# Hedgehog attention into a spectral mode mix: 19 groups of the mix attached to listed iterations of the attention in place of 22 to consecutive ones

## The chip, the cores and the metric

The kernel runs on 1 core of one Trainium2 chip. The metric is the device time of one execution in microseconds (us). Engines: PE is TensorE (matmul; PEld its weight loads), DVE is VectorE, ACT is ScalarE, POOL is GpSimd, SP is SyncE; transfers are issued by SP and POOL and carried by 16 DMA engines. Each engine works through its own queue in order.

## What is computed

Two stages, the second on the result of the first. Shapes: 8 batches, 8 heads, 576 positions, head size 64, model size 512, 64 modes.

```python
def phi(x):                                   # attention with a feature map
    proj = np.einsum('bhsd,df->bhsf', x, w_phi)
    proj = proj - np.max(np.abs(proj), axis=-1, keepdims=True)
    return np.concatenate([np.exp(proj), np.exp(-proj)], axis=-1)
q_p, k_p = (phi(q), phi(k))
kv  = np.einsum('bhsf,bhsd->bhfd', k_p, v)
z   = np.sum(k_p, axis=2)
num = np.einsum('bhsf,bhfd->bhsd', q_p, kv)
den = np.einsum('bhsf,bhf->bhs', q_p, z)[..., None] + 1e-06
x   = num / den                               # heads side by side: 8 x 576 x 512

X = np.fft.rfft(x, axis=1)                    # the spectral mode mix
Xr, Xi = (np.real(X[:, :n_modes]), np.imag(X[:, :n_modes]))
Yr = np.einsum('bmd,mde->bme', Xr, w_r) - np.einsum('bmd,mde->bme', Xi, w_i)
Yi = np.einsum('bmd,mde->bme', Xr, w_i) + np.einsum('bmd,mde->bme', Xi, w_r)
Y[:, :n_modes] = Yr + 1j * Yi
y = np.fft.irfft(Y, n=S, axis=1)
u = x + y
out = u + np.maximum(u @ w_ch, 0.0)
```

`w_r` and `w_i` are 64 matrices of 512 x 512 each, float32: 134 MB to be read, out of the 163.6 MB that the kernel reads in all.

## The kernel before

**Attention.** One loop (L555) over n = 0 to 33. Step n begins the n-th of 32 units `S` (two heads of one batch, or one head of two batches for the first 8), goes on with unit n - 1 (`prev`) and ends unit n - 2 (`old`), all in an order written out by hand. For the present unit: features on PE (`feat_tok`, `feat_q`, `rem_mm`), their maxima on DVE (`absmax`, `mkq`), exponentials on ACT (`exps`, `ekq`), v scaled on POOL (`vscale`, tile `vaug`). For `prev`: `kv_mm`, `num_mm` on PE, the division on DVE (`numer`), which writes x in bfloat16 into `xs_all`. For `old`: `x_mm`, the forward transform on PE, which ACT copies into one of two tiles, `XT0` or `XT1` (L369). In steps 28 to 33 a first part of x W (`flip_early`, `times_w_early`) is added for 6 of the 40 blocks of x.

**Which unit fills which tile.** Units 0 to 3 fill `XT1`, 4 to 7 `XT0`, 8 to 15 (g = 1) `XT1`, 16 to 23 (g = 2) `XT0`, 24 to 31 (g = 3) `XT1`; unit n is written in step n + 2.

**Mode mix.** 32 groups (L108). Groups 0 to 7 take 16 modes of 64 input rows each; groups 8 to 31 take 8 modes `gi` of 128 input rows, g = 1, 2, 3. `weights(k)` (L156) issues a group's `wr` and `wi` from POOL, read as float32 and written as bfloat16 (two transfers of 1 MB written, or four of 0.5 MB for groups 0 to 7), into one of `NW = 3` buffers. `mode_mm(k)` (L390) multiplies (16 or 32 matmuls of 512 columns, `wr` first), `mode_sum(k)` (L424) adds the result to `Yacc` on DVE, or, for g = 3, writes the sum `yst`. `after` (L111) is the last unit that a group's tile needs.

In the loop, a step that has a group does `mode_mm` at its end; the next step does `mode_sum` near its start and then issues the weights of the group three further on:

```python
            while k_in < min(k_out + NW, 2 if n < 3 else 32):   # L585
                weights(k_in)
                k_in += 1
```

On POOL these issues stand behind `load_qk` (q and k of two units, in odd steps 5 to 25) and in front of `vscale` of the step; `wr` waits until PE has read the old `wr` of that buffer, `wi` likewise. `wchb` (`w_ch`) is loaded by POOL in step 16; v (`vn`) by SP two steps ahead.

**Which step has which group** (L622): group k goes to the first step that is free from `after[k] + 2` on, while k < 22. That is groups 0 to 7 in steps 5 to 12, 8 to 15 in 17 to 24, 16 to 21 in 25 to 30.

**After the attention** (L785) a loop over the groups left, k = 22 to 31. For each: the issue of weights three further on, `mode_mm`, `mode_sum`; for g = 3 a `times_w`, four transposes of `yst` (`ptY`, copied to `sY`), and with every odd `gi` `by_batch` (`psZY`, whose copies to `zy` by ACT and DVE are done in the pieces that follow, L717). Then `pieces(plan[k])`: each piece is a `flip_x` (transposes of a pair of blocks of x, `pt`, copied by DVE to `sT`) and a `times_w` (8 matmuls, `psW`, copied by ACT to `xw`), 17 pairs in all. Then up to two `reordered` (L685: `psX` on PE, copied back to `xs_all` by ACT), for k <= 24 and for even k, 11 in all; a block is reordered only after it was flipped. For k = 30 one `times_w` more closes the list; for k = 31 `add_xw` (`psB`) goes ahead of `mode_mm`.

**The end** (L841): 20 units of output: matmuls that add x W, Y W and the inverse transform in PSUM, ReLU on ACT (L762), sum on DVE (L776), in part POOL (L780), and the stores.

Of the kernel before, what the change touches and what calls it, by code (L numbers as in the profile page):

```python
# [26 lines left out]
def kernel(  # L27
# [63 lines left out]
    def qk_pair(pool, i):  # L91
        return [pool.tile([128, 2, 10, D_], BF16, name=f"{nm}2_{i}") for nm in "qk"]
# [18 lines left out]
    after = [3] * 4 + [7] * 4 + [15] * 8 + [23] * 8 + [31] * 8  # L111
    W = {}

    def load(st, which="qkv"):
        for nm, src, bufs in (("q", q, 2), ("k", k, 2), ("v", v, 4)):
            if nm not in which or (nm != "v" and st["n"] >= 2):
                continue
            pool = pa_in if nm == "v" else pa_first
            t = pool.tile([128, 9, D_], F32, name=f"{nm}n", tag=f"{nm}n", bufs=bufs)
            if "bs" in st:  # L120
                for x in range(2):
                    nc.sync.dma_start(  # L122
                        t[64 * x:64 * x + 64],
                        src[st["bs"][x], st["h"]].rearrange("(p j) d -> p j d", j=9))
            else:
                b, g = st["b"], st["g"]
                nc.sync.dma_start(
                    t, src[b, 2 * g:2 * g + 2].rearrange("h (p j) d -> (h p) j d", j=9))
            st[nm] = t


    def load_qk(m):
        st = S[2 * m]
        for nm, src, t in zip("qk", (q, k), qk2s[m % 3]):
            if "bs" in st:
                for x in range(2):
                    b = st["bs"][x]
                    nc.gpsimd.dma_start(
                        t[64 * x:64 * x + 64, :, 0:9, :],
                        src[b:b + 3:2, st["h"]].rearrange("u (p j) d -> p u j d", j=9))  # L140
            else:
                b, g = st["b"], st["g"]
                nc.gpsimd.dma_start(
                    t[:, :, 0:9, :],
                    src[b:b + 2, 2 * g:2 * g + 2].rearrange("u h (p j) d -> (h p) u j d", j=9))
            for x in range(2):
                S[2 * m + x][nm + "b"] = t[:, x]

    def casts(st, eng, which="qk"):
        n = st["n"]  # L150
        for nm, t in zip("qk", qk2s[0]):
            if nm in which:
                st[nm + "b"] = t[:, n % 2]
                eng.tensor_copy(t[:, n % 2, 0:9, :], st[nm])
# [39 lines left out]
    def feat_tok(st, nm, tag):  # L194
        ps = psum.tile([128, 2, 4, 128], F32, name=f"ps{nm}", tag=tag, bufs=1)
        for c in range(4):
            for jj in range(2):
                r = slice(64 * jj, 64 * jj + 64)
                nc.tensor.matmul(ps[:, jj, c, :], lhsT=st[nm + "T"][r, c, :], rhs=w2[r, :],  # L199
                                 start=True, stop=True)  # L200
        st["ps" + nm] = ps
# [248 lines left out]
    def zeros(i):  # L450
        for z in (0, 32, 64):
            nc.vector.memset(XTs[i][:, z:z + 16, :], 0.0)
# [71 lines left out]

    psY = None
    k_in = k_out = 0
    K_IN_ATTN = 22
    pa_last_cm = None
    with tc.manual_schedule():
        load(S[0], "qk")  # L530
        setup()
        load(S[0], "v")
        load(S[1])
        zeros(1)
        casts(S[0], nc.vector)
        casts(S[1], nc.gpsimd, "q")
        load_qk(1)
        for t in AAs:
            nc.gpsimd.memset(t[:, 0, :, 1152:1216], 1.0)
        for t in e2s:  # L540
            nc.gpsimd.memset(t[64:128, :, NCH - 1:NCH], 1.0)
        casts(S[1], nc.gpsimd, "k")

        pa_first_cm.__exit__(None, None, None)
        pa_last_cm = tc.tile_pool(name="pa_last", bufs=1)
        pa_last = pa_last_cm.__enter__()
        qk2s[2] = qk_pair(pa_last, 2)
        for t in qk2s[2]:
            nc.gpsimd.memset(t[:, :, 9, :], 0.0)
        load_qk(2)  # L550
        weights(0)
        k_in = 1
        transp(S[0], "q")
        transp(S[0], "k")
        for n in range(N + 2):  # L555
            cur = S[n] if n < N else None
            prev = S[n - 1] if 0 <= n - 1 < N else None
            old = S[n - 2] if 0 <= n - 2 < N else None
            nxt = S[n + 1] if n + 1 < N else None
            if n + 2 < N:  # L560
                load(S[n + 2])
            if cur:
                feat_tok(cur, "k", "pB")
                feat_q(cur)
            if psY is not None:
                mode_sum(k_out, psY)
                psY = None
                k_out += 1
            if cur:
                rem_mm(cur)  # L570
                absmax(cur, "k")
                absmax(cur, "rem")
                exps(cur, "q")
            if nxt:
                transp(nxt, "q")
            if prev:
                kv_mm(prev)
                kv_cp(prev)
            if cur:
                ekq(cur, "k")  # L580
            if n < 4:
                vscale(cur)
            if n % 2 == 1 and 5 <= n < N - 5:
                load_qk((n + 5) // 2)
# [3 lines that stand above are left out]
            if n in (1, 3):  # L588
                load_qk((n + 5) // 2)
            if n == 16:  # L590
                nc.gpsimd.dma_start(wchb, moe_w_ch.rearrange("(dc p) e -> p dc e", p=128))
            if cur and n >= 4:
                vscale(cur)
            if nxt:
                transp(nxt, "k")
            if cur:
                exps(cur, "k")
                exps(cur, "rem")
            if prev:
                num_mm(prev, 1)  # L600
                numer(prev, 0)
                num_mm(prev, 0)
                numer(prev, 1)
                numer(prev, 2)
            if old:
                x_mm(old)
            e = n - (N + 2 - N_EARLY)
            if e >= 0:
                sTe = flip_early(e)
            if cur:  # L610
                feat_tok(cur, "q", "pA")
                absmax(cur, "q")
                ekq(cur, "q")
            if n == 0:
                forward_matrix()
            if n == 2:
                zeros(0)
            if 10 <= n < 10 + NCH:
                inverse_matrix(n - 10)
            if e >= 0:  # L620
                times_w_early(e, sTe)
            if k_out < K_IN_ATTN and n >= after[k_out] + 2:  # L622
                psY = mode_mm(k_out)
    if psY is not None:
        mode_sum(k_out, psY)
# [157 lines left out]
    u0 = dict(bc=((0, 0), (0, 1)), half=False, late=False, tags=("T2", "T3"))  # L783

    with tc.manual_schedule():  # L785
        plan = {22: 3, 23: 3, 24: 2, 25: 2, 26: 2, 27: 1, 28: 2, 29: 1, 30: 1, 31: 0}
        while k_out < 32:
            k = k_out
            gi = groups[k][1]
            while k_in < min(k_out + NW, 32):  # L790
                weights(k_in)
                k_in += 1
            if k == 31:
                add_xw(u0)
            yst = mode_sum(k, mode_mm(k, "T3"), pb)
            k_out += 1
            if yst is not None:
                if ahead:
                    times_w()
                if gi % 2 == 0:  # L800
                    sY = pb.tile([128, 4, 2, 128], BF16, name="sY", tag="sY")
                for a, b, tag in ((0, 4, "T3"),) if k < 31 else ((0, 2, "T0"), (2, 4, "T1")):
                    pt = psum.tile([128, b - a, 128], BF16, name="ptY", tag=tag)
                    for dc in range(a, b):
                        nc.tensor.transpose(pt[:, dc - a, :], yst[dc], ident_b)
                    nc.vector.tensor_copy(sY[:, a:b, gi % 2, :], pt)
                if k == 31:
                    add_x(u0)
                if gi % 2 == 1:
                    by_batch(sY, gi // 2)  # L810
            pieces(plan[k])
            if k <= 24 or k % 2 == 0:
                assert not copies
                for tag in ("T0", "T1"):
                    if reorder:
                        reordered(tag)
            if k == 30:
                times_w()
        assert not todo and not ahead and not reorder and not copies
# [67 lines left out]
```

## Time and profile before

| what | value | where from |
|---|---|---|
| time, median of 3 runs | 456.05 us (455.77 to 456.72) | runs |
| span of the profiled execution | 456.7 us | page |
| busy: PE, DVE, ACT, POOL | 66%, 64%, 57%, 44% | page, part 1 |
| POOL's DMA queue: bytes written | 76.75 MB | page, part 3 |
| read from HBM, written to it | 163.64 MB, 9.44 MB | page |
| step 5, 10, 11, 21, 31 begin (`psT`) | 53.7, 94.0, 114.6, 196.2, 312.9 us | trace |
| groups 8, 21, 22, 30, 31 begin on PE | 170.7, 310.4, 331.1, 402.8, 415.6 us | trace |
| `wi` of groups 19, 22, 30, 31 lands | 291.2, 322.2, 404.6, 414.4 us | trace |
| waits of PE for `wi` at L416 | 29.6 us, 12 times | waits |
| waits of PE for `wr` at L416 | 8.7 us, 3 times | waits |
| from the end of group 31 (416.7 us) to the end | 40.0 us | trace |

How to read it: every time is counted from the first instruction of the profiled execution. A share of busy time is an average over stages; the steps, groups and landings in the lower rows place the stages. A transfer "lands" when its semaphore says so. The granted clock of PE is 1.00 at full speed.

### The profile page before, as it was taken

Reading aid. Unit: us, or ns where it says so; the run is one execution under the profiler, and the core shown is the slowest. Engines: PE = TensorE matmul, PEld = TensorE weight load, DVE = VectorE, ACT = ScalarE, POOL = GpSimd, SP = SyncE. Lnnn points to the kernel's source line nnn. Section 1 sums busy time; section 2 is a strip of 40 time slices with the busy share of each in tenths; the row PEclk is TensorE's granted clock in tenths of the full one; section 3 lists DMA queues with packets and bytes.
Section 4 is the critical chain, followed back from the end, with each engine's and each line's share of the span. In section 5 each row is a group of like instructions: output and inputs, shape, how many; then the busy total and the mean of one; then the engine's idle time right before and its main releaser. Section 6 shows DMA issues by size and latency. Waiting matters only on the chain.

```text
span 456.7 us, 11065 instructions
## 1 busy us (share of the span) xinstructions
PE 301.7 (66%) x4637; PEld 197.6 (43%) x4637; DVE 292.0 (64%) x418; ACT 261.8 (57%) x528; POOL 198.8 (44%) x251
## 2 busy tenths in 40 slices
PE   3476776833767677655555544755578878868993
PEld 2355565622555565544333432433344445433341
DVE  6578789844988779876666472776322273653873
ACT  4576887833686877865545452765334455644662
POOL 3956476445563256553435231443021212100993
PEclk9976899876886769998778595999999999998997
DMA  6999999999999999999999999999999999990697
GB/s 179 195 228 222 225 213 226 221 206 216 221 228 217 230 219 222 224 219 229 218 207 217 218 218 218 207 203 207 207 207 207 207 207 207 207 179 11 223 341 299
DMA packets 84417, 97.70 MB, mean 214 GB/s; under 512 B 3152, under 2 KB 77136, under 8 KB 84368
## 3 DMA queue, kind: packets, MB, share of 16 engines
q0 software_dynamic: 75728, 76.75, 101.1%
q1 hardware_dynamic: 8480, 20.19, 12.8%
q8 instruction: 36, 0.59, 0.5%
q14 instruction: 13, 0.11, 0.1%
q10 hardware_dynamic: 160, 0.07, 0.1%
HBM read 163.64 MB, written 9.44 MB: 379 GB/s over the span
## 4 chain that ended last, share of the span: by engine, by line
DMA 34%; issue 24%; DVE 17%; PE 11%; POOL 7%; ACT 3%; SPq 1%; DVEq 0%; POOLq 0%; ACTq 0%
DMA wi<-in_moe_w_i_dram 29%; DVE mkq L233 6%; DMA wr<-in_moe_w_r_dram 4%; DVE xs_all L336 2%; DVE nd L322 2%; DVE tB L315 2%; POOL vaug L270 2%; PE ptr L184 1%; PE psNB L305 1%; ACT AA L240 1%; PE kvz L286 1%; PE psB L753 1%; DVE of L776 1%; SPq L122 1%; POOL wr L162 1%
## 5 line engine op out<-in xcount | busy, mean ns | idle before, releaser
L270 POOL TENSOR_TENSOR vaug<-vn,ee 128x576 bf16<-128x576 f32 x64 | 72.7, 1155 | 63.3 <-ACT ee L255 50.2
L240 ACT ACTIVATE AA<-psT 128x1024 bf16<-128x1024 f32 x64 | 62.0, 1021 | 43.6 <-PE psT L208 43.1
L262 ACT ACTIVATE e<-mkq 64x4 f32<-64x4 f32 (+1 forms) x128 | 26.3, 206 | 61.5 <-DVE mkq L233 59.2
L244 ACT ACTIVATE AA<-psk 128x1024 bf16<-128x1024 f32 x64 | 61.4, 1010 | 0.0
L162 POOL DMA_DIRECT2D wr<-in_moe_w_r_dram x24 | 21.9, 912 | 86.6 <-PE psY L416 77.8
L416 PEld LDWEIGHTS <-XT 128*32 128x32 bf16 x384 | 17.1, 171 | 56.6 <-issue 46.4
L667 ACT CAST xw<-psW 128x1024 bf16<-128x1024 f32 x17 | 17.2, 1013 | 40.5 <-PE psW L665 34.6
L233 DVE TENSOR_REDUCE mkq<-psk 128x8 f32<-128x1024 f32 x32 | 38.8, 1213 | 0.7 <-PE psk L199 0.7
L233 DVE TENSOR_REDUCE mkq<-psq 128x8 f32<-128x1024 f32 x32 | 38.9, 1217 | 0.4 <-PE psq L199 0.4
L435 DVE TENSOR_TENSOR Yacc<-psY,Yacc 128x512 f32<-128x512 f32 x16 | 11.0, 689 | 42.5 <-PE psY L416 42.5
L416 PE MATMUL psY<-wi,XT 128*32 128x512 bf16 x192 | 18.0, 435 | 28.8 <-DMA wi<-in_moe_w_i_dram 28.8
L286 PE MATMUL kvz<-vaug,AA 64*128 64x65 bf16 x1152 | 29.2, 210 | 11.5 <-POOL vaug L275 9.8
L190 DVE COPY kT<-ptr 128x640 bf16<-128x640 bf16 x32 | 15.7, 492 | 32.5 <-PE ptr L184 32.5
L665 PE MATMUL psW<-wchb,sT 128*128 128x512 bf16 x136 | 33.5, 391 | 2.1 <-ACT xw L667 2.1
L315 DVE TENSOR_TENSOR tB<-psNB,e 128x650 f32<-128x650 f32 x32 | 26.7, 833 | 11.2 <-PE psNB L305 10.6
L305 PEld LDWEIGHTS <-AA 128*128 128x128 bf16 x640 | 29.0, 110 | 9.3 <-issue 8.9
L286 PEld LDWEIGHTS <-AA 64*128 64x128 bf16 x1152 | 25.1, 107 | 15.9 <-issue 11.8
L162 POOL DMA_DIRECT2D wi<-in_moe_w_i_dram x24 | 21.1, 880 | 23.8 <-PE psY L416 20.5
L322 DVE TENSOR_TENSOR nd<-psNA,tB 128x650 f32<-128x650 f32 x32 | 26.7, 835 | 4.1 <-DVE tB L315 0.5
L416 PE MATMUL psY<-wr,XT 128*32 128x512 bf16 x192 | 17.0, 424 | 18.0 <-DMA wr<-in_moe_w_r_dram 8.7
L336 DVE TENSOR_TENSOR xs_all<-nd,rden 128x640 bf16<-128x640 f32 x32 | 28.0, 874 | 1.1
L184 PE MATMUL ptr<-ident_b,k 128*128 128x128 bf16 x160 | 17.9, 257 | 14.8 <-DVE qT L190 12.6
(132 smaller groups left out, 705.4 us busy)
## 6 DMA issues: line engine op xcount, KB each, us to landing
wr<-in_moe_w_r_dram POOLq DMA_DIRECT2D x24, 1024.0 KB, 25.8
wi<-in_moe_w_i_dram POOLq DMA_DIRECT2D x24, 1024.0 KB, 29.4
wr<-in_moe_w_r_dram POOLq DMA_DIRECT2D x16, 512.0 KB, 15.9
wi<-in_moe_w_i_dram POOLq DMA_DIRECT2D x16, 512.0 KB, 19.6
out_dram<-of SPq DMA_DIRECT2D x16, 512.0 KB, 3.8
vn<-in_v_dram SPq DMA_DIRECT2D x24, 288.0 KB, 5.8
q<-in_q_dram POOLq DMA_DIRECT2D x12, 288.0 KB, 19.3
k<-in_k_dram POOLq DMA_DIRECT2D x12, 288.0 KB, 20.0
```

Source lines behind the costliest of these rows:

```text
L162: nc.gpsimd.dma_start(t, w[8 * gi:8 * gi + 8, g * 128:(g + 1) * 128, :].rearrange("m p e -> p m e"))
L233: nc.vector.tensor_reduce(out=o, in_=i, axis=AX.X, op=ALU.max, apply_absolute_value=True)
L240: nc.scalar.activation(AA[:, 0, ab, 0:1024].rearrange("f (x j p) -> f j x p", j=2, p=64), st["psT"].rearrange("f j (x p) -> f j x p", p=64 ...
L244: nc.scalar.activation(AA[:, 1, ab, 0:1024].rearrange("p (c j f) -> p j c f", c=4, j=2), st["psk"], ACT.Exp, scale=sc)
L270: nc.gpsimd.tensor_tensor(out=vaug[:, ab, :, 0:64], in0=st["v"], in1=ee[:, ab, :].unsqueeze(2).to_broadcast([128, 9, D_]), op=ALU.mult,)
L286: nc.tensor.matmul(kvz[:, hh, ab * 65:(ab + 1) * 65], lhsT=AA[r, 1, ab, 128 * j:128 * j + 128], rhs=vaug[r, ab, j, :], start=(j == 0), sto ...
L305: nc.tensor.matmul(p[:, hh, 65 * c:65 * c + 65], lhsT=AA[:, 0, ab, x:x + 128], rhs=kvzF[:, hh, ab * 65:(ab + 1) * 65], start=True, stop=True,)
L315: nc.vector.tensor_tensor(out=tB, in0=st["psNB"], in1=e2.unsqueeze(3).to_broadcast([128, 2, NCH, 65]), op=ALU.mult,)
L322: nc.vector.tensor_tensor(out=nd, in0=st["psNA"], in1=st["tB"], op=ALU.add)
L336: nc.vector.tensor_tensor(out=xo, in0=nd[:, :, :, 0:64], in1=rden.to_broadcast([128, 2, NCH, 64]), op=ALU.mult,)
L416: nc.tensor.matmul(psY[32 * j:32 * j + 32, :], lhsT=XT[:, c0:c0 + 32, m], rhs=wt[ri][:, 2 * j + par, :], start=(par == 0 and ri == 0), sto ...
L665: nc.tensor.matmul(ps[:, x, :], lhsT=sT[:, x, dc, :], rhs=wchb[:, dc, :], start=(dc == 0), stop=(dc == 3))
```

## The change

The rule "the next free step while k < 22" gives way to a list: `at[k]` is the step of group k, for 19 groups; the other 13 come after the attention. Groups 0 to 4 keep steps 5 to 9; group 5 goes from step 10 to 11, 6 from 11 to 13, 7 from 12 to 14; 8 and 9 keep 17 and 18; 10 to 18 go from 19 to 27 to steps 20, 21, 23, 25, 27, 28, 30, 31 and 33; groups 19, 20 and 21 go from steps 28, 29 and 30 to the loop behind. The pieces of x W there are spread as 2 for each of k = 19 to 23, 1 for each of 24 to 30 and 0 for 31 (17 in all); before they were 3, 3, 2, 2, 2, 1, 2, 1, 1, 0 for k = 22 to 31.

```diff
     k_in = k_out = 0
-    K_IN_ATTN = 22
+    at = [5, 6, 7, 8, 9, 11, 13, 14, 17, 18, 20, 21, 23, 25, 27, 28, 30, 31, 33]
...
-            if k_out < K_IN_ATTN and n >= after[k_out] + 2:
+            if k_out < len(at) and n == at[k_out]:
+                assert n >= after[k_out] + 2
                 psY = mode_mm(k_out)
...
-        plan = {22: 3, 23: 3, 24: 2, 25: 2, 26: 2, 27: 1, 28: 2, 29: 1, 30: 1, 31: 0}
+        plan = {k: 2 if k < 24 else int(k < 31) for k in range(k_out, 32)}
```

With these steps groups 14 and 15 (g = 1, `XT1`) are multiplied in steps 27 and 28, when `x_mm` has put g = 3 of batches 0 and 1, or 0 to 2, into the same tile (unit 24 + b is written in step 26 + b): for these batches the two groups multiply the rows of g = 3 with the weights of g = 1. The amount of work is the same.

## The prediction

> **What bounds the kernel now.** I read the 40 slices first, then the chain of waits, then a table of stretches, and last the timeline of the stretch that decides.
>
> ```profile
> DMA  6999999999999999999999999999999999990697
> GB/s 179 195 228 222 225 213 226 221 206 216 221 228 217 230 219 222 224 219 229 218 207 217 218 218 218 207 203 207 207 207 207 207 207 207 207 179 11 223 341 299
> ...
> DMA 34%; issue 24%; DVE 17%; PE 11%; POOL 7%; ACT 3%; SPq 1%; DVEq 0%; POOLq 0%; ACTq 0%
> ```
>
> The DMA engines are full from slice 1 to slice 34 at 203 to 230 GB/s and empty in slice 36 (411 to 422 us); the last slices are the output. No weight transfer waits for compute anywhere: the packets of the POOL queue run without a gap from 10.7 us to 414.1 us. So the kernel is a stream of fixed bytes that ends when `wi` of group 31 lands (414.4 us), and a rest of 456.7 - 414.4 = 42.3 us.
>
> ```profile
> core 0: us, PE busy (x) PEld busy (x) DVE busy (x) ACT busy (x) POOL busy (x), PEclk, DMA share, GB/s
> ...
> 114.60:196.20 81.60, 58.14 (x1107) 43.01 (x1103) 69.09 (x101) 59.14 (x136) 43.82 (x54) 0.84 1.22 223
> 196.20:312.90 116.70, 67.31 (x1154) 45.13 (x1155) 70.10 (x104) 62.77 (x147) 46.41 (x55) 0.84 1.23 215
> ...
> 331.10:405.30 74.20, 59.42 (x629) 33.70 (x629) 31.24 (x40) 34.38 (x35) 12.30 (x14) 1.00 1.24 207
> ```
>
> In the first row the attention paces itself: 10 iterations in 81.6 us, DVE 85% busy. In the second 10 iterations take 116.7 us and DVE falls to 60%: a group hangs on nearly every iteration and PE, in order, stands before `mode_mm` until the weights land (10 waits on `wi`, 27.6 us, 3 on `wr`, 8.7 us in that stretch). The DMA share is the same in all three rows, so these stalls do not cost the stream anything. In the third row PE is 80% busy on groups and pieces, still with a full stream.
>
> ```profile
> 404.63 0.69 PE L416 MATMUL psY<-wi,XT 128*32 128x512 bf16 x8 [1.16 <-DMA wi<-in_moe_w_i_dram]
> 405.26 1.90 PE L665 MATMUL psW<-wchb,sT 128*128 128x512 bf16 x8
> 407.00 0.39 PE L805 MATMUL ptY<-ident_b,yst 128*128 128x128 bf16 x4
> 407.90 0.61 PE L654 MATMUL pt<-ident_b,xs_all 128*128 128x128 bf16 x8 [0.52 <-DVE sY L806]
> 410.29 0.59 PE L692 MATMUL psX<-xs_all,ident_p 128*128 128x512 bf16 x2 [1.79 <-ACT zy L718]
> 410.72 3.22 PE L665 MATMUL psW<-wchb,sT 128*128 128x512 bf16 x8
> 415.04 0.59 PE L753 MATMUL psB<-xw,ident_p 128*128 128x512 bf16 x2 [1.10 <-ACT xw L667]
> 415.56 0.69 PE L416 MATMUL psY<-wr,XT 128*32 128x512 bf16 x8
> 416.08 0.60 PE L416 MATMUL psY<-wi,XT 128*32 128x512 bf16 x8
> ```
>
> Here the stream hands over to compute. Group 30 runs as its weights land (404.6). Group 31's `wr` landed at 409.3 and its `wi` at 414.4, yet its first matmul starts at 415.56: between them PE does the pieces of k = 30, and there it waits 1.79 us for ACT's `zy` copies before the last `reordered` (L692), and the `psW` behind it takes 3.22 us in place of 1.90, since the granted clock is 0.78 from 410 to 412 us and 0.50 from 412 to 414 us. Group 31 ends at 416.7, 2.3 us after its weights.
>
> **The change, part by part.** *The stream.* Bytes, transfers and their sizes stay. Each `weights(k+3)` still waits for `mode_mm(k)`, so what can change is whether the queue ever runs dry. I followed it from iteration 11 (114.6 us before, taken as 113.5 now: groups 0 to 4 keep their iterations, and so does the stall of iteration 10, in which POOL stands before weight issues; only the matmuls of group 5, 112.3 to 114.3 us, move one on). Durations: half a group 5.05 us (landings 347.5, 352.6, 357.6, 362.7), a q and k pair 2.9 us, a `vn` load 0.72 us, `wchb` 2.6 us, by bytes at the same 415 GB/s of reads. This reckoning gives 288.1 us for the landing of group 19 in the kernel before against 291.2 in the trace, from 131.8 us on; I stretch it by the 2% that are missing. An iteration that does not wait takes 7.95 us (148.6 to 196.2 us, six of them, 7.93 each), 2.2 us more in all over iterations 11 to 14; those from 28 on with a group and an early piece 8.95 (iteration 30's 10.1 less its wait). Then:
> - `mode_mm(8)` in iteration 17 at 169.6, issue of group 11; the queue then lasts to 178.6: 9 us to spare;
> - `mode_mm(14)` in iteration 27 at 249, issue of 17; queue to 259.6: 10 us;
> - `mode_mm(16)` in iteration 30 at 275.3, issue of 19; queue to 282.4: 7 us;
> - `mode_mm(17)` in 31 at 284.2, of 20; queue to 292.7: 8 us;
> - `mode_mm(18)` in 33 at 295.9, of 21; queue to 303: 7 us.
>
> It never runs dry, so the stream ends at 414.4 as before: zero. Bound: 1 us either way, half of the two late landings at the end (388.9 and 404.6 came 6.0 and 6.1 us after their forerunners).
>
> *The attention* ends some 35 us earlier (iteration 31 at about 277 against 312.9), all of it hidden by the stream. If that cover were gone, each iteration's slack would be paid. Moved with the groups: 3 x 16 matmuls, 3 sums of 0.69 us on DVE, and the issues of `wr` and `wi` (0.9 us each on POOL), which stand in front of `vscale` of the iteration they moved to, where they wait for a group that ended 0.2 us before. `mode_mm(14)` and `(15)` now also follow ACT's `XT` copy of their own iteration; such waits took 2.6 us in 3 times, under 1 us each, inside iterations with 7 us of slack in the stream: nothing.
>
> *The 13 groups after it.* They start at 297 us in place of 331. A group with two pieces takes 8.5 us from one to the next (332.2 to 340.7 held three), with one piece 6.4 to 7.5 (396.4 to 402.8), the stream gives one each 10.1. So by about group 26 PE waits for every landing. The 17 `flip_x`, 17 `times_w` and 11 `reordered` are all still there; written out loop by loop, the eleventh `reordered` falls in k = 28 instead of 30. Between groups 30 and 31 the order is then `psW`, `ptY`, `pt`, `psW`, `psB`.
>
> *The hand-over.* From group 30 at 404.63: `pt` ends at 408.5, its copy at 409.23 as before; the last `psW` runs 409.3 to 411.2 at 1.9 us, not 410.72 to 413.9. ACT is free at 410.24, copies it 411.25 to 412.3 (1.01); `psB` to 412.9; `wr` to 413.5; `wi` waits for 414.4 and ends at 415.05. Against 416.68 that is 1.6 us. But PE now idles before group 30 (ready at 401, weights at 404.6), and half clock after that would stretch the first `psW` to 3.2 us: then `pt` to 410.1, second `psW` to 412.7, `psB` to 414.4, group 31 done at 415.3 to 415.6: a gain of 1.1. I take 1.2 us, nearer to the lower end. The rest of 40.0 us keeps its instructions and order: zero, unless the clock falls in it (below).
>
> Sum on the execution shown: 456.7 - 1.2 = 455.5. It lies at the top of the runs (455.77 to 456.72); the same difference on the median gives 456.05 - 1.2 = 454.9.
>
> The row on the clock, and a rule beside it: the stretch from 407.7 to 411.1 us, in which PE was busy 1.4 us and never idle for more than 1.8, was followed by 3.4 us at half clock. The Trainium skill (TensorE: Matmul & The Clock Gate, Why this matters for your kernels) asks only that no idle gap between bursts exceed about 3 us. The trace disagrees, a gap of 1.79 us was enough; by the Trainium skill the hand-over would gain the full 1.6 us, 454.5.
>
> **Rivals.** *The clock falls on the last chain.* With `wi` of group 31 awaited, PE has little to do from 411 to 414.4 (1.3 us of 3.4). If the next 3.4 us run at half clock, `wi`, `ptY`, `psA` and the two `psZY` rounds (3.9 us of matmuls to 420.6) lose up to 1.7 us, and 456.1 is what remains; two such stretches give 457.8. For it: the row just named; against: after `psW`, `psB` and `wr` the stretch may hold enough.
>
> *The queue runs dry* (the slower side). Place: the issues of groups 19 and 21, with 7 us to spare after 19 iterations that no longer wait. It decides from 7.95 + 7/19 = 8.3 us an iteration; every 0.1 us above costs 1.9 us in full, as nothing later catches up. At 8.6 us: 5.5 us lost, 1.2 gained, 460.3; at 8.45 some 458. For it: iterations 11 to 14 took 8.1 to 9.0, those from 28 are known only under waits; against: six iterations in a row at 7.93.
>
> *The stream's own end moves.* From 406 to 414 us the rate falls off (162 GB/s from 405 to 410, 83, 23), so the 16 engines finish up to 8 us apart; other issue times may spread them less. At best half of the 3.9 us that this wastes: 453. Nothing in the profile says why it would.
>
> *Nothing but the attention moves:* the hand-over's gain is lost in waits on ACT, 456.
>
> **How the numbers follow.** A difference under 0.2%, 0.9 us, cannot be told from none here. Forecast 0.50 (454.9, own range 454.3 to 455.8), clock 0.19, dry queue 0.17, stream's end 0.08, nothing 0.06. Faster: 0.38 of the forecast's 0.50, and 0.08: 0.46. Same: 0.12, half the clock's case and the last: 0.28. Slower: 0.09 and 0.17: 0.26. Range 453.0 to 458.8: from the stream's best case to a queue dry for some 4 us.
>
> **What would show it.** Right: iterations 12 to 27 near 7.95 us, no weight landing more than 5.3 us after its forerunner, attention's last group near 296, last landing 414 to 415, no `psX` between groups 30 and 31, group 31 ending within 1.2 us of its landing. Wrong: a slice of DMA below 9 between 270 and 310 us, a landing of group 31 later than 415.5, or a granted clock of 0.5 right after 414 us.

## The result, and the profile after

The changed kernel takes 459.43 us (median of 8 runs, 457.61 to 460.58) against 456.5 us for the kernel before (8 runs, 455.68 to 458.57): a ratio of 1.0055, 95% interval 1.0033 to 1.0076. By that ratio it is slower by some 2.5 us. Run a second time beside the kernel before, it gave 1.0068 (1.0039 to 1.0096).

Its profiled execution spans 458.0 us; that run's own time was 459.79, so 1.8 us lie around the span. The span of 456.7 us that the prediction started from therefore belongs among the slowest runs of the kernel before: in its runs beside the experiments the spans lie mostly between 453.5 and 456.4 us.

The 40 slices of the page of the changed kernel:

```profile
DMA  6999999999999999999999999999999999991697
GB/s 177 202 229 220 218 208 218 229 206 228 220 224 223 218 230 218 229 218 226 223 218 229 208 207 175 193 188 207 207 207 207 207 207 207 207 207 26 216 343 301
```

The row of busy tenths looks almost as before: its digit says 9 for any share above 0.9, and in the windows below the share reads 1.24 in full flow and still 1.13 in a dip. The row of GB/s shows the difference: slices 24 to 26 (275 to 309 us) moved 175, 193 and 188 GB/s where the kernel before moved 218, 207 and 203 in that place. The same stretch by windows, of the changed kernel (columns: stretch in us, its length, busy time and instructions of each engine, granted clock, DMA share, GB/s):

```profile
core 0: us, PE busy (x) PEld busy (x) DVE busy (x) ACT busy (x) POOL busy (x), PEclk, DMA share, GB/s
...
270.00:276.00 6.00, 3.91 (x67) 2.76 (x66) 4.69 (x7) 3.75 (x9) 2.47 (x3) 0.95 1.24 206
276.00:280.00 4.00, 2.28 (x65) 1.73 (x62) 2.25 (x3) 3.11 (x7) 1.82 (x2) 1.00 0.84 125
280.00:286.00 6.00, 4.18 (x40) 2.65 (x40) 4.36 (x6) 3.45 (x9) 2.47 (x3) 0.57 1.24 202
286.00:292.00 6.00, 4.52 (x83) 2.67 (x81) 2.60 (x5) 2.16 (x7) 1.81 (x2) 0.86 1.13 182
292.00:300.00 8.00, 4.80 (x48) 2.66 (x49) 2.25 (x4) 1.51 (x3) 1.75 (x2) 1.00 1.24 206
300.00:306.00 6.00, 4.26 (x39) 2.50 (x40) 2.07 (x3) 1.07 (x2) 1.75 (x2) 1.00 1.15 172
```

The kernel before, in three of these stretches:

```profile
276.00:280.00 4.00, 0.16 (x4) 0.00 (x0) 0.00 (x0) 0.00 (x0) 0.94 (x1) 0.50 1.23 220
...
286.00:292.00 6.00, 3.94 (x48) 2.14 (x45) 4.20 (x6) 3.78 (x10) 2.89 (x4) 1.00 1.24 207
...
300.00:306.00 6.00, 4.01 (x95) 2.84 (x95) 2.86 (x6) 4.08 (x11) 1.98 (x3) 1.00 1.23 205
```

The changed kernel has three dips: 276 to 280, 286 to 292, 300 to 306 us. They stand where the weights of groups 19, 20 and 21 are issued (276.8, 288.3 and 298.1 us). Against 207 GB/s they leave out 4.0 x 82/207 + 6.0 x 25/207 + 6.0 x 35/207 = 3.3 us of transfer. The last weights land at 415.8 us in place of 414.4.

Why the issues come that late is in the timeline of PE in a late step without a group (step 29, from 258.0 to 267.7 us, up to the `psk` of step 30; columns: start, time, instruction, and the idle time before it with what ended it):

```profile
261.50 0.71 PE L362 MATMUL psx<-CF,xs_all 128*128 128x256 bf16 x5
263.69 0.38 PE L378 MATMUL pte<-ident_b,xs_all 128*128 128x128 bf16 x4 [1.49 <-ACT XT L369]
264.01 0.40 PE L199 MATMUL psq<-w,qT 64*128 64x128 bf16 x8
264.85 0.81 PE L386 MATMUL psWe<-wchb,sTe 128*128 128x512 bf16 x3 [0.45 <-DVE sTe L380]
267.35 0.61 PE L199 MATMUL psk<-w,kT 64*128 64x128 bf16 x8 [1.69 <-ACT xw L388]
```

`pte` shares the PSUM tag `tx` with `psx` and waits 1.49 us for ACT's `XT` copy; the next step's `psk` shares `pB` with `psWe` and waits 1.69 us for ACT's `xw` copy. A step with an early block of x W takes 10.6, 9.7 and 10.1 us (steps 28, 29 and 30), with a group or without.

And the hand-over, as the prediction showed it for the kernel before:

```profile
405.73 0.70 PE L416 MATMUL psY<-wi,XT 128*32 128x512 bf16 x8 [0.18 <-DMA wi<-in_moe_w_i_dram]
...
410.39 1.90 PE L666 MATMUL psW<-wchb,sT 128*128 128x512 bf16 x8 [0.79 <-DVE sT L658]
413.39 0.59 PE L754 MATMUL psB<-xw,ident_p 128*128 128x512 bf16 x2 [1.10 <-ACT xw L668]
413.91 0.70 PE L416 MATMUL psY<-wr,XT 128*32 128x512 bf16 x8
415.86 0.70 PE L416 MATMUL psY<-wi,XT 128*32 128x512 bf16 x8 [1.25 <-DMA wi<-in_moe_w_i_dram]
417.08 0.72 PE L806 MATMUL ptY<-ident_b,yst 128*128 128x128 bf16 x4 [0.52 <-DVE yst L444]
417.59 0.63 PE L769 MATMUL psA<-xs_all,ident_p 128*128 128x512 bf16 x1
418.58 1.93 PE L706 MATMUL psZY<-wchb,sY 128*32 128x512 bf16 x16 [0.36 <-issue]
420.30 0.64 PE L712 MATMUL psZY<-ident_b,sY 128*32 128x128 bf16 x16
420.73 1.09 PE L706 MATMUL psZY<-wchb,sY 128*32 128x512 bf16 x16
```

No `psX` stands between the groups, `psW` takes 1.90 us, and PE waits for the weights of group 31, which ends at 416.6 us, 0.7 us after they land (before: 2.3 us). But the first `psZY` then takes 1.93 us and the second, the same 16 matmuls, 1.09. The windows of that stretch:

```profile
414.00:417.40 3.40, 1.59 (x18) 0.68 (x18) 0.75 (x2) 0.00 (x0) 0.00 (x0) 1.00 0.11 20
417.40:420.80 3.40, 3.04 (x39) 1.56 (x44) 0.58 (x2) 0.00 (x0) 0.00 (x0) 0.50 0.00 0
```

After 3.4 us in which PE was busy 1.59 us the granted clock is 0.50 for the next 3.4 us, on the chain that leads to the first store. From the end of group 31 to the end it is 41.4 us, not 40.0. So this execution shows +1.42 us of stream (the last landing), -1.55 us of hand-over (0.74 for 2.29) and +1.45 us after group 31, put down to the clock: +1.3 us, which is 458.0 - 456.7.

### The profile page after: what moved, and what is told of

The parts are those of the page before. It is cut to its first block, busy times and chain, and to the rows that moved or that the text cites. A ratio compares the mean times of both kernels' runs of the same rounds, so it can differ in the third digit from the quotient of the medians.

```text
span 458.0 us, 11045 instructions
## 1 busy us (share of the span) xinstructions
PE 312.6 (68%) x4619; PEld 200.3 (44%) x4637; DVE 295.2 (64%) x418; ACT 261.7 (57%) x528; POOL 198.1 (43%) x251
## 5 line engine op out<-in xcount | busy, mean ns | idle before, releaser
L240 ACT ACTIVATE AA<-psT 128x1024 bf16<-128x1024 f32 x64 | 62.0, 1021 | 11.3 <-PE psT L208 10.6
L262 ACT ACTIVATE e<-mkq 64x4 f32<-64x4 f32 (+1 forms) x128 | 26.4, 206 | 62.7 <-DVE mkq L233 60.4
L666 PE MATMUL psW<-wchb,sT 128*128 128x512 bf16 x127 | 39.7, 455 | 4.0 <-ACT xw L668 2.6
L305 PEld LDWEIGHTS <-AA 128*128 128x128 bf16 x640 | 30.3, 113 | 11.0 <-issue 10.6
L208 PE MATMUL psT<-qT,w 64*128 64x512 bf16 x64 | 14.5, 441 | 27.8 <-DVE mkq L233 27.7
L416 PEld LDWEIGHTS <-XT 128*32 128x32 bf16 x384 | 16.1, 175 | 35.2 <-issue 31.3
L658 DVE COPY sT<-pt 128x1024 bf16<-128x1024 bf16 x17 | 11.7, 691 | 23.6 <-PE pt L655 23.6
```

The source lines that it names most:

```text
L240: nc.scalar.activation(AA[:, 0, ab, 0:1024].rearrange("f (x j p) -> f j x p", j=2, p=64), st["psT"].rearrange("f j (x p) -> f j x p", p=64 ...
L262: nc.scalar.activation(e2[64 * jj:64 * jj + 64, hh, 0:NCH - jj], mkq[64 * hh:64 * hh + 64, 1, 5 * jj:5 + 4 * jj], ACT.Exp, scale=2.0)
L305: nc.tensor.matmul(p[:, hh, 65 * c:65 * c + 65], lhsT=AA[:, 0, ab, x:x + 128], rhs=kvzF[:, hh, ab * 65:(ab + 1) * 65], start=True, stop=True,)
L416: nc.tensor.matmul(psY[32 * j:32 * j + 32, :], lhsT=XT[:, c0:c0 + 32, m], rhs=wt[ri][:, 2 * j + par, :], start=(par == 0 and ri == 0), sto ...
L666: nc.tensor.matmul(ps[:, x, :], lhsT=sT[:, x, dc, :], rhs=wchb[:, dc, :], start=(dc == 0), stop=(dc == 3))
```

## Experiments

Two theories. S: the weight queue ran thin, DMA engines stood idle, and the stream ended later. C: PE, waiting for the last weights, fell to half clock just before the chain that nothing hides. Every kernel was compared with the kernel before on the same chip.

**The three last groups sooner, and later.** In the list `at`:

```diff
-... 25, 27, 28, 30, 31, 33]
+... 25, 27, 28, 29, 30, 31]     (denser; run twice)
+... 25, 27, 28, 31, 32, 33]     (later)
```

> The changed kernel with groups 16, 17 and 18 in steps 29, 30 and 31 in place of 30, 31 and 33, so that groups 19 to 21 are issued some 10 us sooner. Theory S (the weight queue ran thin between 276 and 305 us and some DMA engines stood idle): no stretch of 2 us between 270 and 310 us reads below 370 GB/s, the last weights land 1 to 2 us sooner than the 415.8 us of the changed kernel, and the time falls from 1.0055 of the kernel before by some 1.4 us, to 1.002 to 1.003. Theory C (the loss is the half clock on the chain after group 31): the queue fills as well, but the time stays at 1.005 to 1.006. If both share the loss, 1.003.

> The denser list again (groups 16 to 18 in steps 29 to 31), as one corner of a square of two edits: 1.000 to 1.003 of the kernel before.

> The opposite of the denser list: groups 16, 17 and 18 in steps 31, 32 and 33 in place of 30, 31 and 33, so that the weights of group 19 are issued some 10 us later (near 287 us), after those of group 18 have landed (279.9 us). Theory S: POOL's queue has nothing but stands for some 7 us near 280 to 287 us, all of it is paid at the end: last landing 421 to 424 us, time 1.016 to 1.022 of the kernel before. Theory C alone (the stream does not matter at this size): 1.005 to 1.008.

Denser: 1.0011 (0.9997 to 1.0024) and 1.0022 (1.0010 to 1.0035), last landings at 413.8 and 412.9 us. Later: 1.0214 (1.0181 to 1.0246), last landing 424.0 us. The denser list first (its first trace), then the later one, in the same windows:

```profile
276.00:280.00 4.00, 2.32 (x65) 1.76 (x66) 2.25 (x3) 3.07 (x7) 1.81 (x2) 1.00 1.25 208
280.00:286.00 6.00, 4.33 (x48) 2.96 (x52) 4.18 (x6) 3.63 (x10) 2.46 (x3) 0.72 1.24 208
286.00:292.00 6.00, 3.16 (x81) 2.46 (x75) 3.74 (x6) 2.01 (x7) 1.82 (x2) 1.00 1.24 209
```

```profile
276.00:280.00 4.00, 2.23 (x50) 1.91 (x50) 1.65 (x3) 2.66 (x7) 0.00 (x0) 0.74 0.53 88
280.00:286.00 6.00, 4.35 (x40) 2.80 (x40) 3.90 (x6) 3.90 (x9) 2.47 (x3) 0.50 0.02 5
286.00:292.00 6.00, 4.98 (x84) 2.75 (x82) 2.58 (x4) 2.15 (x7) 1.83 (x2) 0.82 0.35 52
```

Three numbers of the list of 19, changed, fill the dips; two, changed, empty the queue for some 9 us. Theory S holds: moving the issue 10 us sooner brings back 0.33% to 0.57% (either run of the denser list against either of the changed kernel), most of the loss; moving it 10 to 11 us later costs 1.5% to 1.6% more, as S said and C did not.

**Shorter late steps, the list as it is.** Four early blocks of x W in place of six, so that steps 28 and 29 have none:

```diff
-    N_EARLY = 6
+    N_EARLY = 4
...
-        plan = {k: 2 if k < 24 else int(k < 31) for k in range(k_out, 32)}
+        plan = {k: 2 if k < 25 else int(k < 31) for k in range(k_out, 32)}
```

> The changed kernel with 4 in place of 6 blocks of x W inside the attention (in steps 30 to 33 in place of 28 to 33) and one pair of blocks more behind it (k = 24 takes 2 pieces). If the early blocks are what makes a late step take 10 us (PE stands before psk for ACT's copy out of the PSUM that psWe shares with it), steps 28 and 29 take about 8 us in place of 10.6 and 9.7, the weights of group 19 are issued near 272.5 us in place of 276.8, and the dips between 276 and 305 us shrink to a third or less: 1.001 to 1.003 of the kernel before. Rival: the late steps are long for another reason (the clock, the group), they stay at 10 us, and so do the dips and 1.005 to 1.006.

1.0013 (0.9992 to 1.0033). Steps 28 and 29 took 7.9 us each, step 30, with an early block and a group, 11.1; in windows of 4 to 10 us none between 270 and 316 us is below 200 GB/s (of 2 us, one reads 193). It ran beside the second run of the changed kernel (1.0068), and the two intervals do not overlap. In its timeline `psk` follows `psq` almost at once:

```profile
261.59 0.40 PE L199 MATMUL psq<-w,qT 64*128 64x128 bf16 x8
262.29 0.40 PE L199 MATMUL psk<-w,kT 64*128 64x128 bf16 x8 [0.30 <-ACT AA L244]
```

The weights of group 19 were issued at 275.3 us, not at 272.5 as expected (this run was 1.6 us behind by step 28), but those of group 18 landed at 282.0. What counts is the distance of the two ("to spare", worked out before rounding):

| kernel | issue of 19 | landing of 18 | to spare | last landing | ratio |
|---|---|---|---|---|---|
| later | 288.3 | 280.9 | -7.4 | 424.0 | 1.0214 |
| changed, again | 277.9 | 279.9 | 2.1 | 416.0 | 1.0068 |
| changed, with the ten matmuls below | 279.7 | 282.0 | 2.2 | 416.6 | 1.0048 |
| changed | 276.8 | 279.9 | 3.1 | 415.8 | 1.0055 |
| early blocks in 30 to 33 | 275.3 | 282.0 | 6.7 | 414.8 | 1.0013 |
| denser, second run | 267.3 | 280.2 | 12.8 | 412.9 | 1.0022 |
| denser | 267.3 | 281.0 | 13.7 | 413.8 | 1.0011 |
| before | 250.5 | 280.9 | 30.4 | 414.4 | 1 |

**Keeping PE busy up to group 31.** Ten matmuls that nobody reads, where PE waits:

```diff
+    def warm(count):
+        ps = psum.tile([128, 2, DMODEL], F32, name="warm", tag="T0")
+        for i in range(count):
+            nc.tensor.matmul(ps[:, i % 2, :], lhsT=ident_b, rhs=xs_all[:, 0, :],
+                             start=True, stop=True)
...
         for ri in range(2):
+            if k == 31 and ri == 1:
+                warm(5)
...
             if k == 31:
+                warm(5)
                 add_xw(u0)
```

> The changed kernel with ten extra matmuls whose result nobody reads: five in front of the x W of the first output unit, where PE waits for ACT, five between the wr and wi halves of group 31, where PE waits for the weights. Theory C: PE counts as busy up to group 31, the granted clock stays 1.0 from 410 to 425 us, the time from the end of group 31 to the first store shrinks by 1.4 us (9.1 to 7.6), and the time falls to 1.002 to 1.003 of the kernel before. Theory S: no change, 1.005 to 1.006; the dips of the stream between 276 and 305 us stay in either case.

> Both edits. If stream and clock are two separate losses of 1.4 us each, their gains add: 2.5 to 3 us below the changed kernel, 0.997 to 1.000 of the kernel before. If only one of them is real, this equals the better one of the two runs alone. If neither, 1.0055.

> The denser list with the ten extra matmuls around group 31. Theory C (half clock after group 31 costs 1 to 2 us on the typical run): 0.002 to 0.004 below the denser list alone of the same call, and the same difference again between the two kernels with the early load. Rival (the clock's phase differs from run to run, so that it is noise): less than 0.0015 in the two comparisons taken together.

On the changed kernel 1.0048 (1.0028 to 1.0067). On the denser list 0.9987 (0.9970 to 1.0005), where the list alone, run beside it, gave 1.0011; the second time 0.9993 (0.9973 to 1.0013) beside 1.0022. The windows around group 31 of the first of these two:

```profile
411.00:414.50 3.50, 3.14 (x24) 1.05 (x22) 0.29 (x1) 0.09 (x1) 0.00 (x0) 1.00 0.25 43
414.50:418.00 3.50, 3.12 (x69) 2.10 (x70) 1.04 (x4) 0.96 (x1) 0.00 (x0) 1.00 0.00 0
```

PE is busy 3.14 of 3.5 us and the clock stays. In all five traces with the extra matmuls it stays after group 31, and the end from there takes 39.9 us; one of the five is of the kernel before (below). Without them, among seven traces of kernels with 13 groups behind the attention, it halves in four (41.4, 41.5, 41.6 and 42.1 us) and stays in three (39.9, 40.0 and 40.0). So half clock in that place is real and goes with 1.4 to 2.1 us, in some runs and not in others; that the matmuls keep it away fits all five traces, which are few. What they are worth in time is less sure: 0.0024 and 0.0029 less in the pairs of the denser list, 0.0010 less with the early load of `w_ch` (below), 0.0007 to 0.0020 less on the changed kernel, in each pair with intervals that overlap. The amount stays between 0.3 and 1.3 us, no closer; C had put it at some 1.4 us.

**The hand-over alone, on the kernel before.** The eleventh `reordered` in k = 28:

```diff
-                for tag in ("T0", "T1"):
+                for tag in ("T0", "T1", "T0")[:2 + (k == 28)]:
```

> The kernel before with the eleventh reordered done for k = 28 in place of k = 30, all else as it was: the hand-over term of the prediction alone. The prediction's step: no psX between groups 30 and 31, group 31 ends within 1.2 us of its weights, 1.2 us gained, ratio 0.997. Theory C adds that a PE that waits for the last weights falls to half clock afterwards, so that most of it is given back: 0.999 to 1.002, with a granted clock of 0.5 in the 5 us after group 31.

> The kernel before with the eleventh reordered moved to k = 28 and the ten extra matmuls that keep PE busy around group 31. If the hand-over is worth 1.2 us and its loss was the clock, as in theory C: 0.997 to 0.998 of the kernel before. If the hand-over is worth nothing: 0.999 to 1.001.

0.9993 (0.9975 to 1.0010) alone, and 1.0025 (1.0005 to 1.0046) with the ten matmuls. The first is not told from no change, and a gain of up to 1.1 us is not excluded. Its timeline says why the gain is small:

```profile
405.61 0.69 PE L416 MATMUL psY<-wr,XT 128*32 128x512 bf16 x8 [0.78 <-DVE sT L657]
406.04 0.69 PE L416 MATMUL psY<-wi,XT 128*32 128x512 bf16 x8
...
411.12 1.90 PE L665 MATMUL psW<-wchb,sT 128*128 128x512 bf16 x8 [0.78 <-DVE sT L657]
414.12 0.59 PE L753 MATMUL psB<-xw,ident_p 128*128 128x512 bf16 x2 [1.10 <-ACT xw L667]
414.64 0.69 PE L416 MATMUL psY<-wr,XT 128*32 128x512 bf16 x8
```

There group 30 does not wait for weights: it starts at 405.61 us behind PE's own pieces, so group 31 ends 1.9 us after its landing (413.9) even without `psX`. The half clock that theory C expected after it does not come. With ten groups behind the attention PE itself is the later one at the end; there the extra matmuls fill no wait for weights, and the kernel with them is, if anything, slower than the one without (1.0025 against 0.9993, run on different chips).

**A second thin place.** The load of `w_ch` in step 5 instead of 16:

```diff
-            if n == 16:
+            if n == 5:
                 nc.gpsimd.dma_start(wchb, moe_w_ch.rearrange("(dc p) e -> p dc e", p=128))
```

> The denser list with the load of w_ch issued in step 5 in place of step 16. In the traces so far the queue runs thin in another place too, from 62 to 68 us, before the weights of group 3 can be issued (0.6 to 3.5 us of stream lost between 40 and 74 us, another amount in each run). w_ch is 2.6 us of stream that can stand there. If that thin place costs the end of the stream: the dip at 64 us is gone, the last landing 1 to 2.5 us sooner than in the denser list (411 to 413 us), ratio 0.002 to 0.005 lower. Rival (it is made up later): no change.

> All three: denser list, w_ch in step 5, ten extra matmuls. If each does what its theory says: 0.994 to 0.997 of the kernel before, faster than both kernels. If the clock is noise, the same as with the early load alone.

1.0001 (0.9983 to 1.0020) and, with the extra matmuls, 0.9991 (0.9974 to 1.0007), beside 1.0022 and 0.9993. But in none of these four traces was the stream thin at 64 us, with the early load or without, and the last landings (412.9 and 413.9 us) are no sooner than the others' (412.9 and 412.8). The first pair differs by 0.0021, the second by 0.0002. Inconclusive. No kernel tried is faster than the kernel before beyond its interval; the denser list with the extra matmuls comes nearest.

## Why the prediction was wrong

It forecast 454.9 us, a gain of 1.2, and gave 0.26 to slower; the ratio is 1.0055, a loss of some 2.5 us.

*"It never runs dry, so the stream ends at 414.4 as before: zero."* This step failed, twice over. First the size: 7 us to spare at the issue of group 19 were 3.1. The issue itself was put at 275.3 and came at 276.8: the attention reached step 28 sooner than reckoned (247.4 us, not 250.9), but then each late step took 10 us, where I had read 8.95 with a group and 7.95 without out of steps that stood before weights. The run with four early blocks shows what made them long. And the queue's end, put at 282.4, was 279.9: the plain reckoning by bytes gave 279.5, and the 2% that I stretched it by were not there. Second the test itself: I took the landing of the last transfer as the moment at which the stream starts to lose. In the trace the rate falls from 276 us on while group 18 lands at 279.9. A landing is that of the slowest of the 16 engines: the 16 completion marks of that transfer in the trace run from 276.1 to 279.9 us. And an issue does not act at once: the first mark of the late `wr` of group 19 came 7.3 to 7.6 us after its issue (changed kernel: 276.8 to 284.4), of which the transfer takes 5.05, so by this estimate some 2.4 us pass first. Counted to the first mark of group 18, the issue came 0.7 and 3.1 us too late in the two traces of the changed kernel and 2.7 us ahead of it in the run with four early blocks, which has no dip worth the name. The third dip this count does not explain: its issue came 2.6 us ahead of the first mark of group 20 (300.7), and 1.0 us was lost all the same. The table above puts the border between 3 and 7 us before the landing. That engines finish up to 8 us apart stood in the prediction, used only for the end of the stream.

*The rival "the queue runs dry"* named the place (issues of groups 19 and 21) and the sign, with 0.17. It was to decide from 8.3 us an iteration, and the 19 steps from 12 to 30 took 8.36 on average; but the loss came with the queue never empty, and not in full: 3.3 us of transfer are missing, the last landing is 1.4 us later. At the end the changed kernel's engines finish closer together (171 GB/s from 410 to 414 us against 53 before). The completion marks of the last transfer run from 407.1 to 414.4 us before, 410.3 on average, and from 412.9 to 415.8 in the changed kernel, 413.9 on average: the 16 engines lost 3.6 us on average, near the 3.3, but the slowest only 1.4, and the slowest alone is paid.

*The hand-over* moved as predicted: no `psX`, the last `psW` at 1.90 us, group 31 within 1.2 us of its landing. Its size looks too large. The 1.2 us came from an execution in which that very stretch had half clock: `psW` took 3.22 us in place of 1.90, and at full clock those 1.3 us would be gone without any change. On the kernel before, the edit alone is worth 0.3 us (-0.5 to +1.1).

*The clock on the last chain*, a rival with 0.19, is there in four traces of seven, at 1.4 to 2.1 us. The row that disagreed with the Trainium skill (TensorE: Matmul & The Clock Gate, Why this matters for your kernels) did so again: there the advice is to leave no idle gap of PE over about 3 us between bursts of matmuls; here a longest wait of 1.25 us, in 3.4 us with 1.59 us busy, was enough.

*The attention and the 13 groups* went as said: the attention's last group at 297 us (296 forecast), steps 12 to 27 at 8.0 us on average, and PE waiting for the landings behind it, from group 21 on rather than 26. None of that is paid. Of the prediction's signs of being wrong, the late landing of group 31 (415.8) and the half clock came, the latter from 417.4 us on; the digit of the DMA row stayed at 9, too coarse to show the dips. One of its readings is off: slice 1 moved 195 GB/s, not 203 or more; nothing rests on it.

Together, as an estimate: about 2 us of stream (1.0055 and 1.0068 against 1.0011 and 1.0022) and up to some 1 us of clock, less a few tenths of hand-over.

## What to carry to other kernels

In a kernel bound by a stream, a change of schedule is free only while every issue comes well before the queue's end, and "well" has to be measured from the engine that empties first, here 4 to 6 us before the landing, plus the time that an issue takes to act, here some 2.4 us. The length of a step that stands before a transfer misled here about its length without that wait: read it from a step that does not wait, or from the sum of the waits inside. And where PE is made to wait just ahead of a chain that nothing hides, part of the gain can come back as half clock.

## What the runs had not been expected to show

The stream has a second thin place, common to all these kernels: groups 0 to 2 fill the three buffers, and group 3 can be issued only after the first group, near 61 us. How thin it is differs from run to run, for the most part with the clock. The second trace of the changed kernel, then that of the changed kernel with extra matmuls; the two programs are the same up to there:

```profile
56.00:62.00 6.00, 4.93 (x110) 3.59 (x110) 5.63 (x8) 4.29 (x13) 3.98 (x6) 0.98 1.21 206
...
64.00:66.00 2.00, 2.00 (x46) 1.75 (x45) 1.67 (x3) 2.00 (x5) 1.76 (x2) 1.00 1.23 205
```

```profile
56.00:62.00 6.00, 4.91 (x91) 3.89 (x87) 4.09 (x8) 5.03 (x11) 2.46 (x3) 0.61 1.20 228
...
64.00:66.00 2.00, 1.75 (x51) 0.97 (x36) 1.46 (x2) 1.57 (x5) 1.43 (x3) 0.97 0.17 59
```

With a granted clock of 0.61 from 56 to 62 us the first group comes later (62.7 us against 59.2) and the stream falls to 59 GB/s for 2 us. The clock is not all of it: in the second trace of the denser list with the extra matmuls it is 0.64 there, and the stream keeps 197 GB/s. Some of the 3 us by which runs of one kernel differ here may come from it; the early load of `w_ch` was meant to tell, and does not.
